# GEGLU feed-forward kernel: ScalarE's early copies and seeds spread out, and the first w_gate transfer issued later

## The chip, the cores and the metric

The kernel runs on one core of one Trainium2 chip. The metric is the time of one execution in device microseconds (us); the time before is 278.99 us, the median of three runs. One further execution was taken by the hardware profiler, and everything below that speaks of rows, waits or a trace comes from that one.

The core's engines run side by side, each in its own program order: TensorE (PE in the profile; PEld is its weight load) multiplies, VectorE (DVE), ScalarE (ACT) and GpSimd (POOL) do elementwise work, SyncE (SP) mostly issues DMAs. ACT can issue DMAs too, from the same instruction stream as its arithmetic. An instruction that needs another engine's result waits for a semaphore, and everything behind it on its engine waits with it.

## The reference

```
x: [32, 32, 1024]   w_gate, w_up: [1024, 3584]   w_down: [3584, 1024]     (bf16)
_gelu(x) = gelu(x, approximate=True)
reference = (_gelu(x @ w_gate) * (x @ w_up)) @ w_down
```

With the first two axes flattened, x has 1024 rows.

## The kernel before, in words

The 1024 rows are two halves of 512 columns of the transposed x: `xt0` and `xt1`, each brought in by a transposing DMA on SP's queue. w_gate comes in strips of 256 columns (`load_gate(c)`, tiles gw), w_up in strips of 512 (`load_up(c)`, tiles uw, the first one in two transfers of 256). Both go through SP's queue in the order in which they are written, except the very first: the upper half of w_gate's strip 0 (`load_gate(0, nc.scalar, 0, KH)`, 256 KB) is issued by ACT.

The first stage makes gate and up for 28 blocks of 128 columns. It does not multiply everything out: seven products of a 2 by 2 block scheme (Strassen in Winograd's form) replace eight, which needs sums of blocks of x (`T1` to `T4`, made by DVE from `xt0` and `xt1`) and of the weights (S1 to S4, by DVE for blocks 0 and 1 and partly 2, by POOL later), and copies in another type of two plain blocks (`C22` by `copy_a22`, `T["B22"]`). The second stage multiplies by w_down in the same manner and is not touched.

PSUM has two rings of four tiles: tag "p" (`psum_p`: the warm-up tiles, later X, the sums that collect four products) and tag "q" (`psum_q`: A for the gate, Y).

Everything is issued in the order in which it is written. At the start, 18 warm-up products of zeros run on PE (`warm[n % 4]`, line 138) until x and w_gate are there. Then eight blocks of the gate ("LEAD") are made ahead of the rest, two at a time:

- `first_product(i)`: four matmuls into A(i), then ACT copies A(i) to E1 in SBUF (line 185; "e" in the profile).
- `second_product(i)`: four more matmuls accumulate into the same A(i), then ACT takes the gelu (line 191; "gl").

So second_product(i) on PE must wait until ACT's copy e(i) has read A(i). `seed(i)` (line 197) is a copy by ACT from E1 back into a PSUM tile X(i), onto which later products are accumulated; `copy_a22(i)` (line 176) is a copy by ACT from a uw tile to C22(i). Both use ACT for some 0.6 us. After the LEAD blocks come four copies of `B22` (line 263), the first products of the up half (line 268: Y(0) and Y(1), four steps k, each with a step of `T1`), and then `ahead()` (one more first_product, one more second_product), sixth, seventh, fourth and third products of blocks 0 and 1, and so on block by block.

In the loop over LEAD the two extra ACT operations are placed behind the pair of second products:

```
for n in range(0, LEAD, 2):
    first_product(n)
    first_product(n + 1)
    second_product(n)
    if n + 2 < LEAD:
        second_product(n + 1)
    if n in (2, 4):
        copy_a22(n // 2 - 1)
        seed(n // 2 - 1)
```

Of the kernel before, what the change touches and what calls it, by code (L numbers as in the profile page):

```python
# [7 lines left out]
ACT = mybir.ActivationFunctionType  # L8
# [4 lines left out]
def kernel(  # L13
# [18 lines left out]
    nc = tc.nc  # L32
# [11 lines left out]
    KH = DT // 2  # L44
# [36 lines left out]
    def load_gate(c, queue, lo=0, hi=DT):  # L81
        if c not in WG:
            WG[c] = gw.tile([P, DT, 2 * P], bf16, name="gw", tag="gw")
        queue.dma_start(
            out=WG[c][:, lo:hi, :], in_=wg_r[:, lo:hi, 2 * c * P : (2 * c + 2) * P]
        )
# [12 lines left out]
    def a11(i):  # L99
        return block(WG, 2, i, 0)  # L100

    def a12(i):
        return block(WG, 2, i, 1)
# [4 lines left out]
    def a22(i):  # L108
        return block(WU, 4, i, 1)

    def product(ps, lhs, rhs, first=True):
        for k in range(KH):
            nc.tensor.matmul(  # L113
                ps,
                lhsT=lhs[:, k, :],
                rhs=rhs[:, k, :],
                start=(first and k == 0),
                stop=(k == KH - 1),
                skip_group_check=True,
            )  # L120

    def psum_p(name):
        return psum.tile([P, NB], fp32, name=name, tag="p")

    def psum_q(name):
        return psum.tile([P, NB], fp32, name=name, tag="q")

    with tc.manual_schedule():
        zt = opool.tile([P, NB], bf16, name="zt", tag="o")
        nc.vector.memset(zt, 0.0)  # L130
        warm = [psum_p("warm") for _ in range(4)]
        table = opool.tile([P, 8], bf16, name="table", tag="o")
        nc.scalar.activation(table, zt[:, 0:8], ACT.Gelu_apprx_tanh)

        nc.sync.dma_start_transpose(out=xt0, in_=xf[0:NB, :])
        load_gate(0, nc.scalar, 0, KH)
        for n in range(NWARM):
            nc.tensor.matmul(warm[n % 4], lhsT=zt[:, 0:P], rhs=zt, start=True, stop=True)
        load_gate(0, nc.sync, KH, DT)
        load_gate(1, nc.sync)  # L140
        load_up(0, 0, 2)
# [33 lines left out]
        def copy_a22(i):  # L175
            nc.scalar.activation(C22[i], a22(i), ACT.Copy)  # L176
# [3 lines left out]
        def first_product(i):  # L180
            A[i] = psum_q("a")
            product(A[i], a11(i), B11)
            if i % 2 == 0:
                E1[i // 2] = ring.tile([P, 2, NB], fp32, name="e1", tag="ring")
            nc.scalar.activation(E1[i // 2][:, i % 2, :], A[i], ACT.Copy)  # L185

        def second_product(i):
            product(A[i], a12(i), B21, first=False)
            if i % 2 == 0:
                GL[i // 2] = half.tile([P, 2, NB], bf16, name="gl0", tag="half")  # L190
            nc.scalar.activation(GL[i // 2][:, i % 2, :], A[i], ACT.Gelu_apprx_tanh)  # L191
# [3 lines left out]
        def seed(i):  # L195
            X[i] = psum_p("x")
            nc.scalar.activation(X[i], E1[i // 2][:, i % 2, :], ACT.Copy)  # L197
# [51 lines left out]
        held = spool.tile([P, 8], f32r, name="held", tag="held", bufs=1)  # L249
        nc.gpsimd.tensor_copy(held, T["T4"][:, KH - 1, 0:8])  # L250

        for n in range(0, LEAD, 2):
            first_product(n)
            first_product(n + 1)
            second_product(n)
            if n + 2 < LEAD:
                second_product(n + 1)
            if n in (2, 4):
                copy_a22(n // 2 - 1)
                seed(n // 2 - 1)  # L260
        done = LEAD
        for k in range(KH):
            nc.scalar.activation(T["B22"][:, k, :], B22[:, k, :], ACT.Copy)
        for i in range(2):
            Y[i] = psum_q("y")
        for k in range(KH):
# [246 lines left out]
```

## Time and profile before

| | |
|---|---|
| median of 3 runs | 278.99 us (278.86 to 279.08) |
| the profiled execution's own time | 279.1 us |
| its span, first to last instruction | 277.3 us |
| PE busy | 271.0 us, 98% of the span |
| DVE busy | 189.3 us, 68% |
| ACT busy | 138.1 us, 50% |
| POOL busy | 88.7 us, 32% |
| DMA, bytes and mean rate | 26.42 MB, 95 GB/s |
| granted TensorE clock | 1.0 |

The busy share is an average over the span. The change touches only the first 25 us, so what matters there is not the shares but which wait ended last at each step, and when. Times in rows are counted from the span's start. A matmul of 512 columns is listed with some 0.38 us though the next one follows sooner, because matmuls are pipelined; so positions of PE are best read from starts.

### The profile page before, as it was taken

How to read it: one execution, taken by the hardware profiler on the slowest of the kernel's cores; microseconds unless marked ns; L12 is line 12 of the kernel's file. 1: busy time of each engine (PE TensorE's matmuls, PEld its weight loads, DVE VectorE, ACT ScalarE, POOL GpSimd, SP SyncE). 2: the span in 40 equal slices, each digit the busy share in tenths (PEclk: the TensorE clock that was granted, in tenths of full speed). 3: DMA queues.
4: the chain of work that ended last, by engine and by line, in shares of the span. 5: the costliest groups of instructions: out<-in, count | busy, mean ns of one | idle time of the engine just before them, and what ended most of it. 6: DMA issues, size and time to landing. Idle time of an engine off the chain costs nothing.

```text
span 277.3 us, 3341 instructions
## 1 busy us (share of the span) xinstructions
PE 271.0 (98%) x1194; PEld 190.2 (69%) x1194; DVE 189.3 (68%) x227; ACT 138.1 (50%) x236; POOL 88.7 (32%) x81
## 2 busy tenths in 40 slices
PE   8899999999999999999999999999999999999995
PEld 3335777778777787777866677774447888888883
DVE  0079955857567576675766655668994999999900
ACT  2478585565665656656565666632100081870311
POOL 0000294646556475554755544510000000000000
PEclk9999999999999999999999999999999999999999
DMA  7998402342072051243520201259702000000221
GB/s 175 281 242 210 154 13 62 92 138 77 0 229 76 0 172 59 75 123 105 154 76 0 76 20 58 83 183 315 254 0 76 2 0 0 0 2 0 96 96 38
DMA packets 40912, 26.42 MB, mean 95 GB/s; under 512 B 9152, under 2 KB 40896, under 8 KB 40896
## 3 DMA queue, kind: packets, MB, share of 16 engines
q1 hardware_dynamic: 40224, 25.82, 31.9%
q10 hardware_dynamic: 672, 0.39, 0.5%
q8 instruction: 9, 0.15, 0.2%
q14 instruction: 7, 0.06, 0.1%
HBM read 22.02 MB, written 2.10 MB: 87 GB/s over the span
## 4 chain that ended last, share of the span: by engine, by line
PE 94%; DMA 3%; ACT 2%; issue 0%
PE x L113 28%; PE x L368 18%; PE y L113 18%; PE a L113 17%; PE y L368 9%; PE z L368 4%; DMA xt<-in_x_dram 3%; PE y L268 1%; ACT gl L191 0%; ACT e L185 0%; ACT c L176 0%; ACT x L197 0%; ACT o_sb L480 0%
## 5 line engine op out<-in xcount | busy, mean ns | idle before, releaser
L113 PE MATMUL x<-T,s 128*128 128x512 f32 x224 | 63.5, 408 | 0.0
L113 PE MATMUL a<-xt,gw 128*128 128x512 bf16 x224 | 52.8, 380 | 1.7 <-DMA xt<-in_x_dram 0.9
L173 POOL TENSOR_TENSOR s<-gw,s 128x512 fp32r<-128x512 bf16 x26 | 30.5, 1173 | 62.7 <-PE y L113 62.0
L113 PEld LDWEIGHTS x<-T,s 128*128 128x128 f32 x224 | 41.7, 188 | 10.8 <-ACT e L212 0.4
L227 DVE TENSOR_TENSOR u<-y,e 128x512 bf16<-128x512 f32 x28 | 19.3, 691 | 34.8 <-ACT e L225 34.2
L169 DVE TENSOR_TENSOR s<-s,gw 128x512 fp32r<-128x512 f32 x28 | 40.7, 1455 | 0.0
L113 PEld LDWEIGHTS <-gw 128*128 128x128 bf16 x224 | 20.0, 98 | 29.8 <-issue 8.1
L216 DVE TENSOR_TENSOR gT<-gl,x 128x512 bf16<-128x512 bf16 x28 | 19.2, 687 | 18.5 <-PE x L113 18.4
L234 ACT ACTIVATE gl<-h 128x512 bf16<-128x512 bf16 x28 | 17.7, 631 | 27.5 <-DVE h L232 27.5
L113 PE MATMUL x<-T,c 128*128 128x512 f32 x112 | 30.2, 393 | 0.0
L113 PE MATMUL y<-B,s 128*128 128x512 f32 x112 | 30.1, 391 | 0.0
L165 POOL TENSOR_TENSOR s<-gw,uw 128x512 fp32r<-128x512 bf16 x25 | 29.3, 1172 | 0.0
L164 POOL TENSOR_TENSOR s<-uw 128x512 fp32r<-128x512 bf16 x25 | 29.1, 1166 | 0.0
L185 ACT ACTIVATE e<-a 128x512 f32<-128x512 f32 x28 | 16.5, 597 | 23.1 <-PE a L113 23.0
L113 PE MATMUL y<-T,s 128*128 128x512 f32 x104 | 27.8, 389 | 0.0
L368 PE MATMUL x<-tc,sc 128*128 128x512 f32 x112 | 25.7, 389 | 0.0
L113 PEld LDWEIGHTS y<-B,s 128*128 128x128 f32 x112 | 21.0, 188 | 4.8
L113 PEld LDWEIGHTS x<-T,c 128*128 128x128 f32 x112 | 20.9, 188 | 4.8 <-ACT e L225 0.5
L368 PEld LDWEIGHTS x<-tc,sc 128*128 128x128 f32 x112 | 21.0, 188 | 4.4
L225 ACT ACTIVATE e<-x 128x512 f32<-128x512 f32 x28 | 16.8, 600 | 14.4 <-PE x L113 14.3
L113 PEld LDWEIGHTS y<-T,s 128*128 128x128 f32 x104 | 19.5, 188 | 4.1
L191 ACT ACTIVATE gl<-a 128x512 bf16<-128x512 f32 x28 | 16.7, 597 | 8.6 <-PE a L113 8.6
(51 smaller groups left out, 319.0 us busy)
## 6 DMA issues: line engine op xcount, KB each, us to landing
gw<-in_w_gate_dram SPq DMA_DIRECT2D x13, 512.0 KB, 4.3
uw<-in_w_up_dram SPq DMA_DIRECT2D x6, 1024.0 KB, 6.5
v<-in_w_down_dram SPq DMA_DIRECT2D x5, 512.0 KB, 3.7
v<-in_w_down_dram SPq DMA_DIRECT2D x4, 640.0 KB, 8.7
v<-in_w_down_dram SPq DMA_DIRECT2D x8, 256.0 KB, 4.4
out_dram<-o_sb SPq DMA_DIRECT2D x15, 128.0 KB, 1.7
uw<-in_w_up_dram SPq DMA_DIRECT2D x2, 512.0 KB, 6.1
gw<-in_w_gate_dram ACTq DMA_DIRECT2D x1, 256.0 KB, 4.1
```

Source lines behind the costliest of these rows:

```text
L113: nc.tensor.matmul(ps, lhsT=lhs[:, k, :], rhs=rhs[:, k, :], start=(first and k == 0), stop=(k == KH - 1), skip_group_check=True,)
L164: engine.tensor_tensor(S1[i], a21(i), a22(i), ALU.add)
L165: engine.tensor_tensor(S3[i], a11(i), a21(i), ALU.subtract)
L169: nc.vector.tensor_tensor(S2[i], S1[i], a11(i), ALU.subtract)
L173: engine.tensor_tensor(S4[i], a12(i), S2[i], ALU.subtract)
L185: nc.scalar.activation(E1[i // 2][:, i % 2, :], A[i], ACT.Copy)
L191: nc.scalar.activation(GL[i // 2][:, i % 2, :], A[i], ACT.Gelu_apprx_tanh)
L216: nc.vector.tensor_tensor(gT[:, i, 0:NB], GL[i // 2][:, i % 2, :], X[i], ALU.mult)
L225: nc.scalar.activation(e3, X[i], ACT.Copy)
L227: nc.vector.tensor_tensor(U1[i], Y[i], e3, ALU.add)
L234: nc.scalar.activation(G1[i], h1, ACT.Gelu_apprx_tanh)
L368: nc.tensor.matmul(ps, lhsT=lhs[:, i, t * P : (t + 1) * P], rhs=rhs[:, i, :], start=(first and j == 0 and i == 0), stop=(last and j == JF ...
```

## The change

In the prologue, ACT's issue of the first w_gate transfer moves into the warm-up loop, behind a small copy by ACT (8 columns) that reads the PSUM tile of the fourth warm-up product and so waits for it. In the LEAD loop, the pairs copy_a22 and seed behind the second products of n = 2 and n = 4 are taken apart: copy_a22(0) now comes right behind the pair of first products of n = 2, seed(0) behind that of n = 4, seed(1) behind that of n = 6, all ahead of the second products of the same n; copy_a22(1) comes behind the four copies of B22. The instructions of PE, DVE, POOL and SP keep their order. ACT has one instruction more, the small copy.

```diff
@@ -133,9 +133,11 @@
         nc.scalar.activation(table, zt[:, 0:8], ACT.Gelu_apprx_tanh)
 
         nc.sync.dma_start_transpose(out=xt0, in_=xf[0:NB, :])
-        load_gate(0, nc.scalar, 0, KH)
         for n in range(NWARM):
             nc.tensor.matmul(warm[n % 4], lhsT=zt[:, 0:P], rhs=zt, start=True, stop=True)
+            if n == 3:
+                nc.scalar.activation(table, warm[n][:, 0:8], ACT.Copy)
+                load_gate(0, nc.scalar, 0, KH)
         load_gate(0, nc.sync, KH, DT)
         load_gate(1, nc.sync)
         load_up(0, 0, 2)
@@ -249,18 +251,19 @@
         held = spool.tile([P, 8], f32r, name="held", tag="held", bufs=1)
         nc.gpsimd.tensor_copy(held, T["T4"][:, KH - 1, 0:8])
 
+        between = {2: lambda: copy_a22(0), 4: lambda: seed(0), 6: lambda: seed(1)}
         for n in range(0, LEAD, 2):
             first_product(n)
             first_product(n + 1)
+            if n in between:
+                between[n]()
             second_product(n)
             if n + 2 < LEAD:
                 second_product(n + 1)
-            if n in (2, 4):
-                copy_a22(n // 2 - 1)
-                seed(n // 2 - 1)
         done = LEAD
         for k in range(KH):
             nc.scalar.activation(T["B22"][:, k, :], B22[:, k, :], ACT.Copy)
+        copy_a22(1)
         for i in range(2):
             Y[i] = psum_q("y")
         for k in range(KH):
```

## The prediction

> **What bounds the kernel now.** I read the page first (PE busy 98%: only PE's few gaps are to be won), then the chain that ended last, in order of time, for the first 30 us; columns are start, length, what.
>
> ```profile
> 0.74 7.21 DMA xt<-in_x_dram
> ...
> 7.99 7.26 PE a L113 x32
> ...
> 15.27 0.60 ACT gl L191
> 15.87 0.52 ACT c L176
> 16.39 0.49 ACT x L197
> 16.88 0.52 ACT e L185
> ...
> 19.37 0.60 ACT gl L191
> 19.97 0.52 ACT c L176
> 20.48 0.49 ACT x L197
> 20.98 0.52 ACT e L185
> ...
> 22.56 1.83 PE y L268 x8
> 24.39 1.74 PE a L113 x8
> ```
>
> The chain starts with x's first transposing DMA, goes to PE, and leaves PE twice for the same ACT sequence: gelu, copy_a22 (c), seed (x), then the copy e that PE needs before second_product(4), and again before second_product(6). Behind 22.56 it stays on PE, so what PE gains here it keeps unless a new wait takes it.
>
> Then the timeline of PE and DVE around it; in brackets the idle time before a group and who ended it.
>
> ```profile
> 7.99 9.13 PE L113 MATMUL a<-xt,gw 128*128 128x512 bf16 x40 [0.93 <-DMA xt<-in_x_dram]
> 17.45 3.61 PE L113 MATMUL a<-xt,gw 128*128 128x512 bf16 x16 [0.32 <-ACT e L185]
> 21.54 1.02 PE L113 MATMUL a<-xt,gw 128*128 128x512 bf16 x4 [0.48 <-ACT e L185]
> 24.23 1.90 PE L113 MATMUL a<-xt,gw 128*128 128x512 bf16 x8
> 20.47 2.50 DVE L155 TENSOR_TENSOR T<-xt,xt 128x512 fp32r<-128x512 bf16 x4 [1.92 <-DMA xt<-in_x_dram]
> 22.89 2.35 DVE L155 TENSOR_TENSOR T<-xt,T 128x1024 fp32r<-128x1024 bf16 x2
> ```
>
> The two PE waits on e are the target. The DVE rows are the next limit: T1 cannot start before x's second half lands, and DVE then runs T1, T2, T3, T4 without a gap until 29.78.
>
> Last, the DMA answer for the start: bytes per queue (q1 is SP's, q10 ACT's) in three stretches, 2.1 to 4.8, 4.0 to 4.6 and 4.8 to 7.2 us.
>
> ```profile
> q1 hardware_dynamic: 1309, 0.34, 55.4%
> q10 hardware_dynamic: 523, 0.26, 39.0%
> ...
> DMA packets 465, 0.18 MB, mean 297 GB/s; under 512 B 234, under 2 KB 465, under 8 KB 465
> ...
> DMA packets 2702, 0.69 MB, mean 288 GB/s; under 512 B 2700, under 2 KB 2702, under 8 KB 2702
> ```
>
> All of ACT's gate transfer (0.26 MB) moves while x is short of its later 288 GB/s: in 2.7 us x gets only 0.34 of its 1.05 MB.
>
> **Part 1: copies and seeds.** The added waits are none; four ACT operations of 0.59 to 0.62 us move. ACT starts one 0.49 to 0.52 us behind the other when nothing waits.
>
> PE's steps are 0.216 us per matmul ((3.61 - 1.90)/8 = 0.214, with the starts 17.45 and 20.68 over 15 steps 0.2155). The timeline has first_product(4) starting at 15.22, held by strip 2 of w_gate landing. Eight matmuls take PE to 16.95; it starts again at 17.45. With ACT free, e(4) starts when first_product(4) ends (its fourth matmul starts at 15.22 + 3 x 0.216 = 15.87 and lasts 0.38; ACT reacts in 0.04, as at 9.05), 16.30, and takes 0.59 to 16.89; PE reacts 0.05 later, at 16.95. No wait is left: 0.49 us gained. (The pairs without extra ACT work, n = 0 and 2, show the same fit.) The second wait: sixteen matmuls from 17.45 end at 20.90, PE starts at 21.54, 0.64 us; e(6) goes the same way. So second_product(6) starts at 16.95 + 16 x 0.216 = 20.41, 1.13 us earlier.
>
> Does ACT fit them elsewhere? copy_a22(0) starts 0.49 behind e(3) (13.55), at 14.04; its uw strip landed at 13.37. gelu(2), ready at 14.41, starts 0.15 later, gelu(3) at 15.27 as before. seed(0) follows e(5) at 17.65, seed(1) follows e(7) at 21.1; gelu(4) and gelu(6) start some 0.15 late, and their tiles A(4) and A(6) are asked for only 3 us and 2 us later. copy_a22(1) lengthens the B22 group (2.18 us) by 0.52: from gelu(6) at 21.63, B22 runs 22.1 to 24.3 and copy_a22 to 24.8; behind it wait e(8), gelu(7) and the copy E2(0) that seventh_product(0) needs. E2(0) is ready to start when sixth_product(0) ends, about 26.3, and e(8) and gelu(7) are through at 26.05. So this costs nothing, with 0.25 us to spare.
>
> **What is late next.** Y's eight matmuls would start at 20.41 + 4 x 0.216 = 21.27, but take T1 piece by piece. T1's pieces start every 0.605 us ((22.89 - 20.47)/4) and last 0.69: they end at 21.16, 21.77, 22.37 and 22.97. PE's last pair so starts at 22.97 + 0.05 = 23.02 and the next product at 23.02 + 2 x 0.229 (the chain's 1.83/8) = 23.48, against 24.23. **0.75 of the 1.13 us arrive; 0.38 us turn into a wait for T1.**
>
> Further on, every PE step is 0.75 earlier while DVE keeps its times. seventh_product(0) reaches T3's second half at about 27.5, which is made at 27.51: up to 0.05 lost. The two sums h on DVE stay behind the gT products, which keep DVE busy from 29.7 without a gap until 34.1; the first goes from 34.38 to 34.06, h(1) from 35.76 to 35.45 (it waits for one gelu on ACT), and the first_product that takes Y(1)'s tile would start at 36.15 against 36.14 + 0.05. E2(2) likewise just meets PE at 37.87. Each is within 0.05 us and the same wait, so I book zero and keep 0.1 for the range. Later ACT, DVE and POOL are 50 to 68% busy, and the lead stays.
>
> **Part 2: the gate transfer.** ACT's new copy waits for the fourth warm-up product: its weight load stands at 2.44 in the timeline and the longest warm-up product lasts 0.63, so the copy starts at about 3.1 (0.21 us long by the table row), and the DMA issue behind it at 3.15 rather than 1.17, 2.0 us later. Behind these on ACT nothing is due until e(0) at 9.05. PE's eighth warm-up product reuses that tile at 1.19 + 7 x 0.427 = 4.18, when the copy is done. Landing: 4.1 us after issue (page) makes 7.25; x lands at 7.95, so the gate half is still early by 0.7. Were it later, the products' own waits for w_gate strips (0.32 us until 15.2: 7.26 less 32 x 0.217) and the new 0.38 us at T1 would cover another 0.7. Cost zero.
>
> What it does to x is the open term, because all SP transfers behind x, with x's second half and hence T1, move with it. Before, at 4.8 us x has 1.05 - 0.34 = 0.71 MB to go, at 288 GB/s until 7.28. After, x runs alone until the gate's packets come at 3.15 + 1.68 = 4.83 (2.85 before), then shares: 0.26 MB of gate beside 0.13 of x (the row of 4.0 to 4.6 has 231 packets of 512 B against 234 of 256 B), 0.39 MB at 297 GB/s, 1.32 us; then the rest alone.
> - Best: alone from 2.8 at 288 GB/s x has 0.68 MB by 4.8; 1.32 + (0.37 - 0.13)/0.288 = 2.15 us more, end at 6.95: 0.3 us earlier.
> - Worst: x gets no more than 0.34 MB by 4.8, as before: 1.32 + 0.58/0.288 = 3.33, end at 8.13: 0.85 later.
> - Taken: the second transpose's first 2.7 us (15.3 to 18.0 us), which moved 2064 small packets, 0.53 MB, with 0.5 us of near standstill in it (15 to 30 GB/s) and no transfer of ACT's beside it. 1.32 + 0.39/0.288 = 2.67, end at 7.47, 0.2 later; it also had the tail of a w_gate strip beside it (0.09 MB), so I take half, **0.1 us later**. It is the nearest row: same instruction, size and queue.
>
> The Trainium skill speaks against this part: "DMA: Bandwidth & Descriptors", "Issuing engines are not separate DMA queues", says that transfers of all issuing engines interleave on the same 16 DMA engines, so a delay only reorders. By that alone the shift would be zero and the sum 0.75 us.
>
> **Sum.** Against the profiled execution, 279.1 (span 277.3 and 1.8 around it): 279.1 - 0.75 + 0.1 = 278.45. The median of the runs is 0.11 lower: 278.99 - 0.65 = 278.34, say **278.35 us**.
>
> **Rivals.**
> - *x flows better without company* (best case above): T1 and all strips 0.3 earlier, 278.99 - 1.05 = 277.95. For it: q10's packets in 2.8 to 4.8 fall together with x's poorest stretch (a dip to some 90 GB/s). Against: the second transpose dips without them.
> - *The transfer loses idle wire time*: x and T1 0.4 to 0.85 later, which eats the gain: 278.6 to 279.1. For it: below 2.8 us x alone reached only 125 GB/s, so the engines may have been idle for lack of descriptors. Against: its 288 GB/s later.
> - *Slower: transpose and copy disturb each other.* Place: the shared stretch from 4.8. If it runs at the 90 to 160 GB/s seen near 3.3 us, where q10 joined, and not at 297, 0.39 MB take 2.4 to 4.3 us rather than 1.32, so x and T1 are 1.1 to 3 us late beside the 0.1: 279.5 to 281.4. It decides above 1.3 us of lateness (0.75 + 0.56). Against: 4.0 to 4.6 had both at full rate.
> - *The waits are not ACT's copies*: the change then moves nothing, about 279.1. Against it, the chain's lines.
>
> **How the numbers follow.** Forecast (278.2 to 278.55) 0.52; better flow 0.15; lost wire time 0.22; slower 0.08; nothing 0.03. The range 277.9 to 279.0 takes in the forecast, the better flow and most of the lost wire time. A change under 0.2%, 0.56 us, is about what a measurement of this kernel cannot tell from none; faster means below 278.43. The forecast's value lies 0.08 below that bound, so I give it 0.41 below and 0.11 above; with better flow 0.56 faster. Same: 0.11 + 0.22 + 0.03 = 0.36. Slower 0.08.
>
> **What would show it.** PE's two groups at 17.45 and 21.54 lose "ACT e L185" as releaser, and a short PE wait on DVE T at L268 appears; T1's first piece starts at about 20.57, following x's second landing; the first product starts at 8.0 to 8.1 with x, not gw, as releaser; the product behind Y starts near 23.6. Wrong would be: first product behind gw; T1 later than 21.2; or an ACT wait on E2(0) ahead of the seventh products.

## The result, and the profile after

The changed kernel takes 277.61 us (median of 6 runs, 277.56 to 277.72) against 278.92 us before (median of 6, 278.77 to 279.08): 1.31 us less, a ratio of 0.9953 with a 95% interval of 0.994 to 0.9966. The forecast was 278.35 us, 0.6 us less, and its range ended at 277.9. The sign was right, the size was half of what came, and most of the missing half lies in the term that had been booked as a small loss. Measured once more (e8 below), the changed kernel took 277.63 us against 278.72, 1.09 us less; so the gain is 1.1 to 1.3 us.

The chain of the changed kernel, first 30 us (start, length, what):

```profile
0.73 7.18 DMA xt<-in_x_dram
7.96 6.85 PE a L113 x31
...
14.86 6.21 PE a L113 x28
21.07 1.85 PE y L271 x8
22.91 1.74 PE a L113 x8
```

ACT has left it altogether: from x's landing on it is PE alone. PE and DVE in the timeline:

```profile
7.96 13.11 PE L113 MATMUL a<-xt,gw 128*128 128x512 bf16 x59 [0.43 <-DMA xt<-in_x_dram]
22.75 1.90 PE L113 MATMUL a<-xt,gw 128*128 128x512 bf16 x8
19.26 2.50 DVE L157 TENSOR_TENSOR T<-xt,xt 128x512 fp32r<-128x512 bf16 x4 [1.86 <-DMA xt<-in_x_dram]
21.68 2.35 DVE L157 TENSOR_TENSOR T<-xt,T 128x1024 fp32r<-128x1024 bf16 x2
```

All gate products up to Y run without a gap, so both waits on e are gone, and the waits for w_gate strips with them. The product behind Y starts at 22.75 instead of 24.23: 1.48 us, which is 0.03 (an earlier start) + 0.32 (strips) + 0.49 + 0.64 (the two waits on e). Nothing is left for T1 to take, because T1 starts at 19.26 and not at 20.47, 1.21 us earlier. The span falls from 277.3 to 275.8.

A first part of why T1 moved is seen in who issues what at the start. The timeline of the kernel before:

```profile
0.74 5.10 SPq L135 DMA_TRANSPOSE xt<-in_x_dram  x1
1.17 0.46 ACTq L84 DMA_DIRECT2D gw<-in_w_gate_dram  x1
```

And of the changed one:

```profile
0.73 3.79 SPq L135 DMA_TRANSPOSE xt<-in_x_dram  x1
3.19 0.43 ACTq L84 DMA_DIRECT2D gw<-in_w_gate_dram  x1
```

SP is through with x's transposing DMA 1.31 us sooner and issues the strips sooner. The DMA answer for 2.1 to 4.8 us shows x alone on the wire, twice the 0.34 MB of before, and no packet of ACT's queue:

```profile
q1 hardware_dynamic: 2728, 0.70, 114.1%
```

The gate's packets, issued at 3.19, begin only at 5.89, when x's are nearly through (the last one starts at 6.15, against 7.46 before); all of them move in the next stretch, 4.8 to 7.2 us:

```profile
q10 hardware_dynamic: 528, 0.26, 39.6%
```

The second part lies in x's second half, on which T1 waits. Its transposing DMA moved its first packet 0.27 us earlier than before (15.04 against 15.31) but its last one 1.19 us earlier (18.70 against 19.89). In the kernel before its packets all but stopped, 64 in the half microsecond from 16.16, where the changed kernel has some 560; so most of T1's 1.21 us was won there. "The lagging engine", below, follows this up.

### The profile page after: what moved, and what is told of

Its sections match the earlier page's. It is cut to its first block, busy times and chain, and to the rows that moved or that the text cites. A ratio compares the mean times of both kernels' runs of the same rounds, so it can differ in the third digit from the quotient of the medians.

```text
span 275.8 us, 3328 instructions
## 1 busy us (share of the span) xinstructions
PE 270.0 (98%) x1179; PEld 190.5 (69%) x1194; DVE 189.2 (69%) x227; ACT 138.1 (50%) x237; POOL 88.6 (32%) x81
## 4 chain that ended last, share of the span: by engine, by line
PE 96%; DMA 3%; issue 0%; ACT 0%
PE x L113 28%; PE x L371 18%; PE y L113 18%; PE a L113 17%; PE y L371 9%; PE z L371 4%; DMA xt<-in_x_dram 3%; PE y L271 1%; ACT o_sb L483 0%
## 5 line engine op out<-in xcount | busy, mean ns | idle before, releaser
L113 PE MATMUL a<-xt,gw 128*128 128x512 bf16 x212 | 51.0, 380 | 1.1 <-DMA xt<-in_x_dram 0.4
L371 PEld LDWEIGHTS <-gT 128*128 128x128 bf16 x112 | 10.9, 98 | 13.2 <-issue 0.3
```

Of the source, the lines that this page charges most:

```text
L113: nc.tensor.matmul(ps, lhsT=lhs[:, k, :], rhs=rhs[:, k, :], start=(first and k == 0), stop=(k == KH - 1), skip_group_check=True,)
L371: nc.tensor.matmul(ps, lhsT=lhs[:, i, t * P : (t + 1) * P], rhs=rhs[:, i, :], start=(first and j == 0 and i == 0), stop=(last and j == JF ...
```

## The experiments

Theories in the expectations: A, an early ACT transfer holds up SP's transposing DMA; B, only bytes on the shared wire count; C, any ACT transfer issued early breaks in, whatever its size; D, the transposing DMA needs the 16 DMA engines in step, and what throws them out of step stays with the strips behind; E, the lag of one engine in the strips depends on what follows x. All times below are read as in this table: the length of SP's first transposing instruction; when x's completion came; the time between the first and the last of the 16 completions of strip 2 of w_gate ("spread", from the trace's completion events); the start of T1, of the first product and of the product behind Y; the median.

| kernel | SP's instr. | x landed | spread | T1 | first product | behind Y | median us |
|---|---|---|---|---|---|---|---|
| before | 5.10 | 7.95 | 0.97 | 20.47 | 7.99 | 24.23 | 278.92 |
| changed | 3.79 | 7.91 | 0.13 | 19.26 | 7.96 | 22.75 | 277.61 |
| e8, changed again | 3.90 | 7.96 | 0.12 | 19.39 | 8.00 | 22.81 | 277.63 |
| e1, spread alone | 4.86 | 7.71 | 0.96 | 20.19 | 7.75 | 23.31 | 277.91 |
| e2, gate alone | 3.92 | 7.98 | 0.13 | 19.40 | 8.02 | 24.09 | 278.77 |
| e3, gate on SP | 3.77 | 6.62 | 2.05 | 20.71 | 7.97 | 23.84 | 277.91 |
| e4, after 1 product | 3.86 | 8.12 | 0.32 | 19.52 | 8.16 | 22.96 | 277.43 |
| e5, after 9 products | 3.72 | 6.59 | 0.40 | 19.47 | 8.73 | 23.53 | 281.12 (not read, see e5) |
| e6, quarter early | 4.55 | 7.48 | 0.92 | 20.29 | 7.52 | 23.41 | 278.27 |
| e7, gate before x | 4.77 | 8.02 | 0.50 | 20.32 | 8.06 | 23.45 | 278.34 |
| e9, 17 rows early | 4.94 | 9.15 | 0.11 | 20.39 | 9.19 | 23.99 | 278.85 |
| e10, 16 rows early | 4.19 | 8.40 | 0.09 | 19.64 | 8.44 | 23.24 | 278.16 |
| e11, quarters on SP | 3.94 | 6.79 | 1.67 | 20.99 | 7.65 | 24.12 | 278.44 |
| e12, early and late | 4.97 | 9.15 | 0.13 | 19.54 | 9.20 | 24.01 | 278.87 |
| e13, quarter late | 3.79 | 7.40 | 1.54 | 20.43 | 7.68 | 23.55 | 277.97 |

The kernel before took 278.72 to 278.82 beside e1 to e13. Except where a profile is named, the verdict rests on the medians; the other columns are one profiled execution each.

**The two halves apart.** e1 undoes the move of the gate transfer:

```diff
-            if n == 3:
-                nc.scalar.activation(table, warm[n][:, 0:8], ACT.Copy)
-                load_gate(0, nc.scalar, 0, KH)
+        load_gate(0, nc.scalar, 0, KH)      # ahead of the warm-up loop, as before
```

> Only ScalarE's copies and seeds are spread out; the gate transfer is issued at the start, as before. The prediction's own part 1, unchanged: PE's two waits on e go, the up products wait for T1, the product behind Y starts at 23.48, time 0.75 us below before, 278.2. Theory A (the early ACT transfer holds up SP's transposing DMA and everything queued behind it, and the move of that transfer undoes this): the same 278.2, with SP's first instruction at 5.1 us, T1 at 20.5 and a PE wait for T1 of about 0.4 us. Rival B (only bytes on the shared wires count; T1's earlier start in the changed kernel was chance and the gain is all ScalarE's): 277.6 to 277.9, T1 anywhere from 19.3 to 20.5.

Measured 277.91, ratio 0.997 (0.9958 to 0.9981): 0.82 us gained.

```profile
20.19 2.50 DVE L155 TENSOR_TENSOR T<-xt,xt 128x512 fp32r<-128x512 bf16 x4 [1.96 <-DMA xt<-in_x_dram]
20.93 2.54 PE L269 MATMUL y<-T,s 128*128 128x512 f32 x8
23.31 1.90 PE L113 MATMUL a<-xt,gw 128*128 128x512 bf16 x8
```

Y's eight matmuls take from 20.93 to 23.31, 2.38 us (2.02 before), so they wait for T1 as forecast; the product behind them starts within 0.17 us of the forecast 23.48, T1 itself being 0.28 early here. Rival B's T1 is allowed by its width, but its claim that the whole gain is ScalarE's is not: the medians lie 0.3 us apart (277.79 to 278.1 here, 277.52 to 277.72 over the ten runs of the changed kernel), with 278.73 for the kernel before beside e1 and 278.72 beside e8.

e2 does the other half alone:

```diff
-        load_gate(0, nc.scalar, 0, KH)
         for n in range(NWARM):
             nc.tensor.matmul(warm[n % 4], lhsT=zt[:, 0:P], rhs=zt, start=True, stop=True)
+            if n == 3:
+                nc.scalar.activation(table, warm[n][:, 0:8], ACT.Copy)
+                load_gate(0, nc.scalar, 0, KH)
```

> Only the gate transfer moves behind the fourth warm-up product; copies and seeds stay in their pairs. Theory A: SP's first instruction takes 3.8 us, T1 starts near 19.3, PE's waits for w_gate strips (0.32 us) go, its two waits on e (0.49 and 0.64 us) stay: the product behind Y starts at 23.85 to 23.95, time 278.6. Rival B: SP's instruction stays at 5 us, T1 at 20.4 to 20.6, time 278.9 to 279.1.

Measured 278.77 against 278.73, ratio 1.0 (0.9991 to 1.0009): nothing.

```profile
17.29 3.61 PE L113 MATMUL a<-xt,gw 128*128 128x512 bf16 x16 [0.48 <-ACT e L187]
19.40 2.50 DVE L157 TENSOR_TENSOR T<-xt,xt 128x512 fp32r<-128x512 bf16 x4 [1.88 <-DMA xt<-in_x_dram]
21.39 1.02 PE L113 MATMUL a<-xt,gw 128*128 128x512 bf16 x4 [0.48 <-ACT e L187]
24.09 1.90 PE L113 MATMUL a<-xt,gw 128*128 128x512 bf16 x8
```

T1 is 1.07 us earlier, yet PE only 0.14, because the waits on e are still there. Theory A had the DMA side right and PE's side too large by 0.2 us: the wait for strip 2, one of those 0.32 us, comes only behind the product whose gelu starts ACT's sequence, so ACT's sequence ended no sooner without it, and the wait on e widened by what the strip's wait gave up (0.48 against 0.32 at the first of the two). So 0.82 and 0 apart make 1.31 together (1.09 in e8): the early strips and T1 pay only once ACT no longer holds PE.

**Where the gate transfer may stand.** e4 and e5 change `n == 3` to `n == 0` and `n == 8` (e5's copy then reads `warm[n % 4]`).

> As the changed kernel, but the gate transfer is issued behind the first warm-up product (about 1.85 us) instead of the fourth (3.19). Theory A: its issue falls into SP's transposing DMA again, so that instruction takes 4.3 us or more, T1 starts after 19.7, PE waits up to 0.3 us at T1 or at the strips; time 277.8 to 278.3. Rival B: 1.3 us earlier or later changes nothing, 277.6.

Measured 277.43 (0.9955; 0.9943 to 0.9968), not to be told from the changed kernel. ACT's issue came at 2.27, since its copy stands behind ACT's first activation (2.02 to 2.23), and already that is late enough: SP 3.86 us, the gate's packets from 5.85, when x's are nearly through. Theory A's own number for this run (4.3 us or more) failed, and the run by itself agrees with Rival B. Of the issue times tried, 1.17 harms, and 2.27, 3.19 and 4.89 (e5) do not.

> As the changed kernel, but the gate transfer is issued behind the ninth warm-up product, near 5.25 us. Theory A, mended by the run behind one product (an ACT transfer issued once SP's transposing DMA is being worked off gets its turn behind that DMA; no harm to it): SP's first instruction stays at 3.8 us and T1 near 19.3; the gate half lands 0.8 to 1.5 us later than the 7.63 of the changed kernel, the first product starts at 8.4 to 9.1 with gw as releaser, and since the waits for strips and T1 are gone there is little to cover it: time 0.3 to 0.9 us above the changed kernel, 277.8 to 278.5. The prediction's own view (0.7 us of lateness covered by T1 and the strips): no change, 277.6.

In the profiled execution x lands at 6.59, and the first product starts at 8.73, released by w_gate's half strip (gw) and not by x, 0.77 later than in the changed kernel; the product behind Y is 0.78 later. So no lateness is covered there any more, against the prediction's 0.7 us of cover.

```profile
8.73 13.12 PE L113 MATMUL a<-xt,gw 128*128 128x512 bf16 x60 [2.01 <-DMA gw<-in_w_gate_dram]
```

Its four executions took 278.37 (the profiled one), 280.3, 281.95 and 283.35, so the median is not read. What spread them is not shown: in e12, below, PE sat idle for longer before its first product, 2.67 us, and ten executions took 278.78 to 279.05.

**Does ACT's early transfer harm by its bytes?** e6 leaves half of it there, SP does the rest behind x:

```diff
+        load_gate(0, nc.scalar, 0, KH // 2)      # ahead of the warm-up loop
         for n in range(NWARM):
...
+        load_gate(0, nc.sync, KH // 2, KH)
```

> Copies and seeds spread out; ACT issues only a quarter strip (128 KB) at the start as in the kernel before, SP the other quarter behind x. Theory A: harm in proportion to what ACT moves early: SP's first instruction at 4.3 to 4.5 us, between 3.8 and 5.0, time between the changed kernel and the spread alone, 277.6 to 277.9. Rival C (any early ACT transfer breaks into the transposing DMA, whatever its size): 4.8 us or more and 277.9. Rival B: 3.8 us, 277.6.

SP's instruction 4.55 us, between 3.8 and 5.0 as A had it and short of C's 4.8, but the time, 278.27 (0.9982; 0.9973 to 0.9992), is above the spread alone: two matmuls start at 7.52 and PE then waits for SP's quarter until 8.28.

e7 uses one queue: `load_gate(0, nc.sync, 0, KH)` ahead of x's transposing DMA.

> Copies and seeds spread out; SP issues the gate half ahead of x's transposing DMA, ACT nothing at the start. Theory A: one queue, so nothing breaks in: the transposing instruction takes 3.8 us, its data end near 6.8 us, its completion stands behind no gate packets, so x lands at 7.1 to 7.5 and the first product starts then; T1 as in the changed kernel, 19.0 to 19.5, which takes part of the lead back; time 0.2 to 0.6 us below the changed kernel, 277.0 to 277.4. Rival B: as the changed kernel, 277.6.

278.34 (0.9987; 0.9978 to 0.9996), SP's instruction 4.77: Theory A is wrong in saying that a second queue is needed. A transfer ahead of x in the same queue slows it too, and x's packets still came at 720 to 1040 per us between 3.5 and 5.5, when the gate's had all been moved, against 1130 in the changed kernel.

e9 and e10 put a load of almost no bytes in the place of the early transfer, on top of the changed kernel; its data are not used (e10: 16 for 17):

```diff
+        nc.scalar.dma_start(out=xt1[0:17, 0, :], in_=w_gate[0:17, 0:NB])
         nc.sync.dma_start_transpose(out=xt0, in_=xf[0:NB, :])
```

> The changed kernel with a small extra load issued by ACT at the start, at the place of the kernel before's gate transfer: 17 rows of 1 KB, whose count has no divisor that would spread it, so that it should sit on one of the 16 DMA engines; its data are not used. Theory D (x's transposing DMA needs the 16 engines in step; what it finds unevenly loaded when it starts makes it slow, and the unevenness stays with the strips behind it): SP's first instruction at 4.3 us or more, T1 after 19.7, the second transposing DMA dips, time 277.8 to 278.3. Rival C (any ACT transfer issued before x's is under way breaks in): the same here and in the run with 16 rows. Rival B (bytes count; 17 KB are nothing): 3.8 us, T1 19.3, 277.6.

> The same with 16 rows of 1 KB, which spread over the 16 engines evenly. Theory D: as the changed kernel, SP's first instruction at 3.8 to 4.0 us, T1 19.2 to 19.5, 277.6. Rival C: 4.3 us or more, T1 after 19.7, 277.8 to 278.3. Rival B: 277.6.

Timeline of e9:

```profile
0.73 4.94 SPq L136 DMA_TRANSPOSE xt<-in_x_dram  x1
9.19 13.11 PE L113 MATMUL a<-xt,gw 128*128 128x512 bf16 x60 [1.60 <-DMA xt<-in_x_dram]
```

And of e10:

```profile
0.74 4.19 SPq L136 DMA_TRANSPOSE xt<-in_x_dram  x1
8.44 13.11 PE L113 MATMUL a<-xt,gw 128*128 128x512 bf16 x60 [1.16 <-DMA xt<-in_x_dram]
```

17 KB cost as much of SP's time as 256 KB had (4.94 against 5.10) and 1.2 us of the kernel's (278.85, ratio 1.0001). In the trace, x's packets all but stop between 3.5 and 4.0 us (53 in 0.5 us where 560 is the full rate) while 17 packets of 1 KB crawl through, ending in a single completion packet: one engine. That is the slow start which D forecast, and it refutes B; that the transposing DMA needs its 16 engines in step is D's explanation, which no run shows. Spread evenly the load costs a third of that on SP and under half in time (4.19 us, 278.16, ratio 0.9975), but not nothing, so C is right that each early transfer tried breaks in, and wrong that evenness does not matter. D's second half fails here: the spread of the strips is 0.11, no lag.

**The lagging engine.** In the kernel before, 15 of strip 2's 16 completions came by 14.70 and the last at 15.18; in the changed kernel all by 14.01. The trace does not say which engine a completion belongs to. In e1, e3 and e13 too the last one stands apart, 0.48 to 0.91 us behind the 15th; in e6 four are late, and in e11 all are strewn over 1.67 us. e3, e11, e12 and e13 look for what makes one engine lag. e3 issues the half strip on SP behind x, e11 does it in two quarters; neither has an ACT transfer at the start.

```diff
-                load_gate(0, nc.scalar, 0, KH)
+        load_gate(0, nc.sync, 0, KH)      # e11: (0, KH // 2), then (KH // 2, KH)
         load_gate(0, nc.sync, KH, DT)
```

> Copies and seeds spread out; the first half strip is issued by SP behind x's transposing DMA, and no transfer is issued by ACT at the start. Theory A: SP's first instruction at 3.8 us, T1 at 19.2 to 19.5, and x lands before 7.5 since no gate packets stand ahead of its completion; the first product starts between 7.4 and 7.9, time 277.2 to 277.6. Rival B: x's landing and T1 as in the kernel before (20.5), time 278.1 to 278.3.

> Copies and seeds spread out; SP issues the first half strip behind x in two quarters, so that the first two matmuls need only the first. Theory D: x lands near 6.6 (no gate packets of ACT ahead of its completion), the first quarter near 7.3, and PE starts at 7.3 to 7.6, 0.4 to 0.6 us before the changed kernel; T1 takes 0.1 to 0.2 back: 277.2 to 277.4. If one DMA engine lags again, as in the run with the half strip on SP, the strips behind it hold PE and the time lies at 277.6 to 278.3, scattered.

Timeline of e3:

```profile
12.41 9.67 PE L113 MATMUL a<-xt,gw 128*128 128x512 bf16 x44 [0.81 <-DMA gw<-in_w_gate_dram]
20.71 2.50 DVE L155 TENSOR_TENSOR T<-xt,xt 128x512 fp32r<-128x512 bf16 x4 [1.55 <-DMA xt<-in_x_dram]
```

x lands at 6.6 to 6.8, as A had it. But the strips lag by 2.05 and 1.67 us, PE waits 0.81 and 0.63 us for one, and T1 is later than in the kernel before, so A's T1 and time failed, and D's 277.2 to 277.4 with them; what e11's expectation named as the other outcome came, somewhat above its 278.3. Medians 277.91 (277.56 to 278.66) and 278.44 (277.82 to 279.13), scattered. x was not disturbed here, so the lag does not come from that.

e12 keeps the early transfer and lets ACT issue the strip's other half behind the fourth product:

```diff
+        load_gate(0, nc.scalar, 0, KH)      # ahead of the warm-up loop
...
             if n == 3:
                 nc.scalar.activation(table, warm[n][:, 0:8], ACT.Copy)
-                load_gate(0, nc.scalar, 0, KH)
-        load_gate(0, nc.sync, KH, DT)
+                load_gate(0, nc.scalar, KH, DT)
```

> Copies and seeds spread out; ACT issues the lower half of the channels' gate strip at the start, as before, and the other half behind the fourth warm-up product; SP begins with strip 1. Theory D (breaking into x's transposing DMA makes it slow and leaves one engine behind): SP's first instruction at 4.8 to 5.1 us, the 16 completions of strip 3 spread by about 1 us, T1 after 20.1, time 277.9. Theory E (the lag arises where SP's strips follow x's transposing DMA directly, and an ACT transfer behind x levels the engines): 4.8 to 5.1 us as well, but a spread of 0.2 us or less, the second transposing DMA without a dip, T1 at 19.6 to 19.9, time 277.6 to 277.8.

```profile
0.74 4.97 SPq L135 DMA_TRANSPOSE xt<-in_x_dram  x1
9.20 13.11 PE L113 MATMUL a<-xt,gw 128*128 128x512 bf16 x60 [2.67 <-DMA xt<-in_x_dram]
19.54 2.50 DVE L157 TENSOR_TENSOR T<-xt,xt 128x512 fp32r<-128x512 bf16 x4 [1.89 <-DMA xt<-in_x_dram]
```

x is broken into (4.97 us), yet the spread is 0.13 and T1 at 19.54: E's side, not D's. Behind x this run moves the same strips in the same order as the kernel before, and x's data end at nearly the same time (7.32 against 7.46). The first completion of strip 2 comes as it did (14.14 against 14.21), the last at 14.27 against 15.18, and T1 0.93 us earlier: so 0.8 to 0.9 us of T1 go with the late completions and the standstill of the second transposing DMA, which this run does not have either. The time is no better than before (278.87) since x's completion comes at 9.15.

e13 has ACT issue a quarter strip behind the fourth product and SP the other quarter.

> As the changed kernel, but ACT issues only a quarter strip (128 KB) behind the fourth warm-up product, and SP the other quarter behind x. If x's completion standing behind ACT's packets sets PE's start: x lands near 7.5 rather than 7.9, PE starts 0.3 to 0.45 us earlier, T1 takes none of it (0.48 us of room): 277.2 to 277.35. If the start is set otherwise: 277.6. Theory E: strips stay level (spread 0.2 us or less).

x lands at 7.40 and PE starts at 7.68, 0.28 us earlier, but the lag is back (1.54 us), a strip holds PE for 0.47 us and T1 is at 20.43: 277.97, scattered from 277.57 to 278.68, and not 277.2 to 277.35. E's "an ACT transfer behind x levels the engines" holds for 256 KB and not for 128.

No version beat the changed kernel beyond what the runs can tell.

## Why the prediction was wrong

**Part 1 held.** Alone it gave 0.82 us for the 0.75 forecast (95% interval 0.5 to 1.2), some of it because T1 happened to start 0.28 us earlier in e1 than in the kernel before. Both waits on e went, their 0.49 and 0.64 us are in the sum of the changed kernel, the moved copies cost nothing, and in e1 PE waited at Y for T1, the named next limit.

**The step that failed is what the gate transfer does to x** and to the transfers behind it, taken as 0.1 us later with bounds of 0.3 earlier and 0.85 later. Measured, x's last packet started 1.31 us earlier (6.15, not 7.46), and T1, which that shift was to move, started 1.21 us earlier (19.26, where 20.57 was forecast). Against the spread alone the move is worth 0.3 us by the medians (277.91 to 277.61), and 0.56 at the product behind Y in the profiled executions (23.31 to 22.75; e1's, at 278.1, was its slowest): 0.27 in waits for strips (13.38 against 13.11 for the gate products) and about 0.5 in waits for T1, less 0.21 because the first product started later than in e1. Three assumptions in it were wrong:

- *Who shares.* The gate's packets were put 1.68 us behind their issue and in turns with x's. Issued at 2.27 or 3.19, they came only when x's were nearly through. The prediction also drew on "DMA: Bandwidth & Descriptors", "Issuing engines are not separate DMA queues", in the Trainium skill, which says that transfers of all issuing engines interleave on the same 16 DMA engines. That a delay only reorders was the prediction's own conclusion from it, and it was not enough: e9 shows an order in which 17 KB cost 1.2 us.
- *What the row of 2.1 to 4.8 us meant.* Without the gate's packets beside it x was taken to move 0.53 MB in these 2.7 us, or 0.68 at best; it moved 0.70. The gate's own 0.26 MB, at 297 GB/s, are 0.88 us of the 1.31 (an estimate from the rows of the prediction), and these now stand behind x, ahead of the strips; the other 0.4 us is a disturbance beyond its bytes, which e9 and e10 show with next to no bytes. The near standstill of the second transpose, taken as proof that x dips without company, had company of another kind. It stands in the runs with late completions (before, e1, e3, e6, e11, e13: 41 to 108 packets in the poorest half microsecond) and is absent where the spread is under 0.2 us (555 or more); e4, e5 and e7, at 0.32 to 0.50, have 534, 402 and 294.
- *That everything behind x moves with x's end.* T1 went with the slowest completions. In strip 2 the first completion moved by 0.33 us (14.21 to 13.88), the last by 1.17 (15.18 to 14.01), and T1 by 1.21. So some 0.3 us of T1's gain came with x's earlier end, and some 0.9 with the late completions gone, as in e12. That larger part has no term in the prediction.

That x landed near the forecast (7.91, the first product at 7.96) was luck: its data were through by 6.2, but its completion stood behind the gate's. x lands at 6.6 with no ACT packets there (e3, e5), 7.40 with 128 KB, 7.91 with 256 KB. "DMA: Bandwidth & Descriptors", "Queues, rings and completion order", in the Trainium skill says just this: a completion lands only after every earlier write of its engine, across queues.

**A term left out.** PE's 0.32 us of waits for strips were used as cover for lateness; with earlier strips they were a gain, and they are in the 1.48 us. The cover was an argument for one sign only.

Open: what makes completions lag, and so the cause of the larger part of T1's move. In these traces, one for each kernel, it went with the order behind x, level (spread 0.09 to 0.32 us) where 256 KB of ACT's followed x directly, and was not derived from anything; nor is it shown why an issue at 1.17 breaks in and one at 2.27 does not.

## What to carry to other kernels

When a wait is removed on one engine, list the later ones that the move also reaches and ask for both signs of each: here ACT's copies, the strips and T1 hid one another, and two halves worth 0.82 and 0 made 1.1 to 1.3. Before pricing two transfers by their bytes, look at the issue length of the first on its queue and at the spread of the 16 completions: the last completion sets the wait. And a transfer issued behind a transposing DMA can delay that DMA's completion even where it does not slow its data.

## What the runs showed of the hardware

- A transposing DMA of 1 MB takes SP 3.7 to 3.9 us undisturbed; 17 rows of 1 KB on one DMA engine at its start make that 4.94, 16 rows over all of them 4.19.
- The last of the 16 completions of a strip comes 0.9 to 2 us behind the first in some orders of issue (before 0.97, e3 2.05), and 0.1 us behind it in others (the changed kernel 0.13, e12 0.13); in the former the second transposing DMA all but stops (64 packets in half a microsecond before, 87 in e3, against some 560).
- x's data, through by 6.1 to 6.2 us, counted as landed at 6.62 with no packets of ACT's behind them (e3), at 7.40 with 128 KB (e13) and at 7.91 with 256 KB (the changed kernel).
